# Six steps of a fused scan and feed-forward kernel: eight products in place of seven, the halves of y placed round them, and a chunk's first transposes moved

## The chip, the cores and the metric

The kernel runs on one core of a Trainium2 chip. Its time is the device time of one execution in microseconds (us), the median over several runs. A separate execution is recorded by the hardware profiler; all views below come from that one. The engines are TensorE (PE; its weight loads are shown apart as PEld), VectorE (DVE), ScalarE (ACT), GpSimd (POOL) and SyncE (SP, which here only issues DMAs). Each engine works through its own queue in the order in which the program emitted the instructions, and waits where an operand is not ready or a buffer is not free.

## The reference

Two blocks in a row. The first is a chunked state-space scan over 4 sequences of 8 heads, 768 positions, head width 32 and state width 16; the second is a feed-forward layer over the 3072 x 256 result.

```python
def _attn_ref(x, a, B, C):
    log_a = np.log(np.clip(a, 1e-06, 1.0))
    for c in range(nc):
        ...
        L = np.exp(cum[:, :, :, None] - cum[:, :, None, :]) * causal
        M = np.einsum('bhin,bhjn->bhij', Cc, Bc) * L
        y_intra = np.einsum('bhij,bhjd->bhid', M, xc)
        y_inter = np.einsum('bhin,bhnd->bhid', Cc, state) * decay_to_i[:, :, :, None]
        y[:, :, sl] = y_intra + y_inter
        ...
        state = decay_full[:, :, None, None] * state + np.sum(Bx, axis=2)

def _moe_ref(x, w_in, w_out):
    h = x @ w_in
    g = h * np.cos(h)
    return (g @ w_out).astype(np.float32)
```

d_model is 256 and d_ff 2048; everything is float32.

## The kernel before

**Steps and chunks.** The sequence is cut into 6 chunks of 128 positions (`NC = 6`). For each chunk the feed-forward layer runs 16 steps (`NF = 16`). Step n = 16c + f belongs to chunk c and place f. A step takes half of the chunk's rows (512 columns in all) and 256 of the 2048 hidden columns, computes h for them in one PSUM bank called `hp`, applies the cosine, and three steps later (`LAG = 3`) multiplies the gated result into the output accumulator `o`.

**One step's engines.** TensorE makes hp(n). ScalarE turns it to whole turns k (`wind_k`, L685), VectorE takes the rest w (`wind_w`, L691), ScalarE applies the sine (`gate`, L700), VectorE multiplies hp by it and writes gT (`gated`, L705). After that hp's bank may be written again. From n = 16 on, POOL forms differences gd of gT's quarters (`differ`, L730 to L733). The output product of step n (`seven(n)`, L849) uses seven products of 128 x 128 blocks instead of eight, after Strassen's scheme in Winograd's form, with gT, gd and prepared differences of w_out.

**Seven or eight products for hp.** `first(n)` (L678) makes hp with four matmuls of 256 columns, as much work as eight products of 128. `begin7(n)` (L778) makes it with seven: three products first; then ScalarE copies three parts (`copies`, L782 and L783); then two more products (`rest7[n][0]`), which wait for the copies; then VectorE adds the parts up (`sums` within it, L786 and L788); the last two products (`rest7[n][2]`) are made in the next step, behind the sums. They need differences of w_in (`wid`, POOL, L749) and of y (`differ_y`, POOL, L760). Before the change the steps in `sevens`, n = 33 to 93, all use seven.

**The order in such a step** is written out in `period7(n)`. On TensorE: `begin7(n)`, the first two products of `seven(n - 3)`, the last two hp products of n - 1, the middle part of `seven`, `rest7[n][0]`, the rest of `seven`. On VectorE: `wind_w(n - 1)`, the sums of n, `gated(n - 1)`, and then whatever `scan_work(c, f)` hands over as `extra`. A step that does not use seven, but is followed by one that does, leaves its `gate` and `gated` to the next step (`late`).

**PSUM.** There are eight banks: two for `o`, two tagged "h" used in turn by hp, and two pairs (`pair`) used by the scan. `bank_of(n)` says which steps take a bank of a pair for hp instead of an "h" bank: a third bank, f in (2, 6, 9, 10, 15) for chunks 2 to 4. Two steps that follow each other in the list of "h" users use different banks, and the next one waits for the first of them to be released.

**The scan in between.** While chunk c is in the feed-forward layer, chunk e = c + 1 is scanned, piece by piece. The pieces are: transposing blocks of B and C (`turn_blocks`, L585, VectorE), masking C (`mask_c`, L592, ScalarE), decays along the positions (`reaches`, L575, and `decays0`, L376, scans on VectorE), C weighted by them (`reach_c`, tile rT, L597), the products of C and B (`inner2`, L614, TensorE, into both pairs), their weighting by the decays (`weights`, tile m, L466, VectorE, one call for a quarter), the products of state and C (`open2`, L628, into both pairs again as ys), the sums for the next state (`sums2`, L478), the products with x (`finish2(e, (k,))`, L643, for the half k of the chunk), their copy to yT (`take_y`, L652, ScalarE), and the state's update (`add_state`, L501 for part 0, L503 for part 1). `sums2`, `take_ahead` (L490) and the decay scans of chunk e + 1 do not exist for the last chunk, e = 5. `open2` uses the states after half-chunks 2e - 1 and 2e, and `add_state(2e, (1,))` makes the second.

**Where the pieces stand.** `visits(n, e)` gives step f = 5 `inner2` ahead of everything on TensorE and three of four `weights` ahead of `wind_w`; step f = 12 `open2`; step f = 13 `sums2` ahead, `finish2(e, (0,))` in the middle, and two quarter scans. Step f = 14 has `finish2(e, (1,))` ahead. `scan_work` holds the rest; for c = 2 it has a list of its own, since chunk 3's first transposes stand at f = 0 there.

Of the kernel before, what the change touches and what calls it, by code (L numbers as in the profile page):

```python
# [25 lines left out]
def kernel(  # L26
# [18 lines left out]
    NC = S // P  # L45
    DM, DF = moe_w_in.shape
    KT = DM // P
    NF = DF // P
# [1022 lines left out]

    sevens = range(2 * NF + 1, NC * NF - 2)
    late = set()

    def bank_of(n):

        c, f = divmod(n, NF)
        third = n % 3 == 1 if c == NC - 1 else f in (2, 6, 9, 10, 15)  # L1080
        return pair("hp")[:, 0] if third else bank([P, TB], "hp", "h")

    def gates(n):
# [8 lines left out]
        gate(n)  # L1092
        gated(n)

    def period7(n, extra=(), begin=(), mid=(), early=(), o_first=False):

        first_, then, last_ = seven(n - LAG)
        for do in begin:
            do()
        if o_first:  # L1100
            first_()
        begin7(n, bank_of(n))
        while finished:
            finished.pop()()
        if not o_first:
            first_()
        if n - 1 in sevens:
            rest7[n - 1][2]()
            wind_k(n - 1)
        for do in mid:  # L1110
            do()
        then()
        rest7[n][0]()
        for do in early:
            do()
        if n - 1 in sevens:
            wind_w(n - 1)
        rest7[n][1]()
        if n - 1 in sevens or n - 1 in late:
            gate(n - 1)  # L1120
            gated(n - 1)
        last_()
        for do in extra:
            do()
# [53 lines left out]
    for n in range(AHEAD, 2 * NF):  # L1178
        c, f = divmod(n, NF)
        if n < NC * NF:  # L1180
# [33 lines left out]
            if joins:  # L1214
# [5 lines left out]
            behind += [lambda at=at: turn_blocks(*at) for at in chunks_at(n, "turn")]  # L1220
            behind += [lambda k=k, p=p: decays0(k, p) for k, at in unit_at.items()
                       for p in range(2) if at[0][p] == n]
            behind = [lambda k=2 * c + i, q=q: weights(k, q) for c, i in chunks_at(n, "weigh")
                      for q in range(2)] + behind
            behind = [lambda k=k: weights(k, 1) for k in units_at(n - 1, 3)] + behind
# [49 lines left out]
            sums2(c + 1)  # L1275
        load_more(n)

    def visits(n, e):

        f = n % NF  # L1280
        if f == 5:
            return dict(o_first=True, begin=[lambda: inner2(e)],
                        early=[lambda: weights(2 * e, 0), lambda: weights(2 * e + 1, 0),
                               lambda: weights(2 * e, 1)])
        if f == 12:
            return dict(mid=[lambda: open2(e)])
        if f == 13:
            return dict(o_first=True, begin=[lambda: sums2(e), lambda: take_ahead(e)],
                        mid=[lambda: finish2(e, (0,)), lambda: take_y(e, 0)] + [
                            lambda i=i: differ_y(e, i, G, slice(0, 1)) for i in range(4)],  # L1290
                        early=[lambda i=i: half_decay(2 * e + 3, 0, i)
                               for i in range(2 if e < NC - 1 else 0)])
        return {}

    def half_decay(k, p, i):

# [7 lines left out]
    def scan_work(c, f):  # L1304
# [6 lines left out]
                3: [lambda: reaches(e, 1), lambda: mask_c(e, 1, 1)],  # L1311
                4: [lambda: reach_c(e, 0), lambda: reach_c(e, 1)],
                6: [lambda: weights(2 * e + 1, 1), lambda: add_state(2 * e, (0,))],
                7: [lambda: add_state(2 * e, (1,))],
                11: [lambda: turn_blocks(e + 1, 0, (1,))],
                12: [lambda: turn_blocks(e + 1, 0, (0,))]}
        for i in range(2 if e < NC - 1 else 0):
            work.setdefault(13 + i, []).append(lambda i=i: half_decay(2 * e + 3, 1, i))
        if c == 2:
            work[0] = [lambda: add_state(5), lambda: turn_blocks(e, 0)]  # L1320
            work[1] = [lambda: turn_blocks(e, 1, (1,)), lambda: mask_c(e, 0, 0),
                       lambda: mask_c(e, 0, 1)]
            work[2] = [lambda: turn_blocks(e, 1, (0,)), lambda: mask_c(e, 1, 0),
                       lambda: mask_c(e, 1, 1)]
            work[3] = [lambda: reaches(e, 0)]
            work[4] = [lambda: reaches(e, 1)]
            work[6] = [lambda: weights(2 * e + 1, 1), lambda: reach_c(e, 0)]
            work[7] = [lambda: add_state(2 * e, (0,))]
            work[8] = [lambda: reach_c(e, 1)]
            work[9] = [lambda: add_state(2 * e, (1,))]  # L1330
        for i in range(4 if e < NC - 1 else 0):
            work.setdefault(7 + i, []).append(lambda i=i: half_decay(k, i // 2, i % 2))
        if e == NC - 1:
            for i in (11, 12, 15):
                work.pop(i)
        return work.get(f, [])

    for n in range(2 * NF, NC * NF + LAG):
# [9 lines left out]
        if n >= NC * NF:  # L1348
            second(n - LAG)
        elif n in sevens:  # L1350
            at = visits(n, e) if live else {}
            if f == 14 and c >= 2 and c < NC - 1:
                at = dict(o_first=True, begin=[lambda: finish2(e, (1,)), lambda: take_y(e, 1)])
            period7(n, extra, **at)
        else:
            first(n, rest7[n - 1][2] if n - 1 in sevens else None, to_=bank_of(n))
            if n - 1 in sevens:
                gates(n - 1)
            wind(n)
            for do in extra[:1]:  # L1360
                do()
            shut(n)
            for do in extra[1:]:
                do()
            second(n - LAG)
# [40 lines left out]
```

## Time and profile before

| what | value |
|---|---|
| median of 3 runs | 363.54 us (363.39 to 363.96) |
| the profiled execution, whole | 364.01 us |
| its span from first to last instruction | 361.6 us |
| TensorE matmul, steps with seven products, mean length of one instruction | 277 ns (two instructions to a product) |
| matmul of `first`, 256 columns | 383 ns |
| w, VectorE (L691) | 687 ns |
| k, ScalarE (L685) | 598 ns |
| sine, ScalarE (L700) | 722 ns |
| gT, VectorE (L705) | 686 ns |
| gd on POOL, first of three (L730) | 804 ns |
| granted TensorE clock | 1.0 throughout |

A line of the timeline gives the start and the length in us, then the engine, the source line, the operation, the tile written and the tiles read, the shape, and how many instructions are merged; in square brackets, how long the engine had been idle and what ended that. In the view by window, a line gives the window in us, its length, then busy us and instruction counts of PE, PEld, DVE, ACT and POOL, the granted clock, the share of the DMA engines and GB/s. TensorE's bars overlap, so its waits are read from the distance between starts.

### The profile page before, as it was taken

The numbers are of one execution on the slowest core, as the hardware profiler recorded it, in microseconds if no ns is written. First come the engines' busy times: TensorE is split into PE (matmuls) and PEld (weight loads), VectorE is DVE, ScalarE is ACT, GpSimd is POOL, SyncE is SP. The second block draws the span as 40 slices with busy tenths as digits, with TensorE's granted clock in tenths as the row PEclk, the third lists the DMA queues.
The fourth block names the chain that finished last, engine by engine and source line by source line (L and its number), as shares of the span: only waits on it lengthen the run. The fifth ranks groups of instructions, "written<-read, shape, count | busy, mean of one in ns | idle before, by whom it ended". The sixth has DMA issues, their size and how long they took to land.

```text
span 361.6 us, 10733 instructions
## 1 busy us (share of the span) xinstructions
PE 353.6 (98%) x4268; PEld 329.6 (91%) x4268; DVE 273.4 (76%) x479; ACT 213.0 (59%) x446; POOL 251.9 (70%) x410
## 2 busy tenths in 40 slices
PE   7999999999999999999999999999999999999995
PEld 4788888889989999998999999999999989999995
DVE  7789998478777847989868888868887536666663
ACT  3587766544455357456656656666746746666651
POOL 6567757879869987974866865766775674685671
PEclk9999999999999999999999999999999999999999
DMA  7996947692676129021319212101001001001011
GB/s 143 293 344 142 221 93 122 114 127 60 131 107 112 40 62 133 17 54 33 73 35 132 33 25 52 23 14 29 0 2 32 2 2 33 2 0 31 2 29 29
DMA packets 97328, 26.46 MB, mean 73 GB/s; under 512 B 87328, under 2 KB 93184, under 8 KB 97280
## 3 DMA queue, kind: packets, MB, share of 16 engines
q1 hardware_dynamic: 96032, 25.41, 35.0%
q8 instruction: 33, 0.54, 0.6%
q10 hardware_dynamic: 1248, 0.39, 0.5%
q14 instruction: 15, 0.12, 0.1%
HBM read 22.38 MB, written 3.34 MB: 71 GB/s over the span
## 4 chain that ended last, share of the span: by engine, by line
PE 81%; DVE 10%; ACT 4%; issue 1%; DMA 1%; POOL 1%; SPq 0%; DVEq 0%; POOLq 0%; ACTq 0%
PE o L849 28%; PE hp L778 21%; PE hp L678 17%; PE o L808 7%; DVE w L691 2%; DVE gT L705 2%; ACT w L700 2%; PE y L643 2%; DVE m L466 1%; DMA bc<-in_B_dram 1%; DVE rT L597 1%; DVE lam L376 1%; ACT k L685 1%; PE y L628 1%; PE y L478 1%
## 5 line engine op out<-in xcount | busy, mean ns | idle before, releaser
L700 ACT ACTIVATE w<-w,quarter 128x512 f32<-128x512 f32 x96 | 69.3, 722 | 67.9 <-DVE w L691 67.4
L730 POOL TENSOR_TENSOR gd<-gT 128x256 f32<-128x256 f32 x79 | 63.5, 804 | 65.3 <-DVE gT L705 53.1
L691 DVE SCALAR_TENSOR_TENSOR w<-hp,k 128x512 f32<-128x512 f32 x96 | 65.9, 687 | 55.8 <-ACT k L685 55.2
L685 ACT ACTIVATE k<-hp 128x512 int32<-128x512 f32 x96 | 57.4, 598 | 35.0 <-PE hp L678 25.3
L705 DVE TENSOR_TENSOR gT<-hp,w 128x512 f32<-128x512 f32 x96 | 65.9, 686 | 16.0 <-ACT w L700 10.4
L849 PE MATMUL o<-words,gd 128*128 128x128 f32 x474 | 76.6, 277 | 0.0
L678 PE MATMUL hp<-yT,w_in 128*128 128x256 f32 x280 | 66.8, 383 | 0.3 <-DVE gT L705 0.3
L849 PEld LDWEIGHTS o<-words,gd 128*128 128x128 f32 x474 | 64.1, 192 | 0.5
L778 PE MATMUL hp<-m,wid 128*128 128x128 f32 x366 | 61.7, 277 | 0.2 <-ACT hp L783 0.2
L678 PEld LDWEIGHTS hp<-yT,w_in 128*128 128x128 f32 x280 | 51.4, 190 | 8.0 <-POOL mag L250 0.7
L778 PEld LDWEIGHTS hp<-m,wid 128*128 128x128 f32 x366 | 50.6, 192 | 0.7 <-ACT hp L783 0.3
L849 PE MATMUL o<-w_out,gT 128*128 128x128 f32 x316 | 50.1, 277 | 0.2 <-issue 0.2
L778 PE MATMUL hp<-yT,w_in 128*128 128x128 f32 x244 | 47.2, 275 | 0.4 <-DVE gT L705 0.4
L849 PEld LDWEIGHTS o<-w_out,gT 128*128 128x128 f32 x316 | 43.3, 192 | 1.9 <-issue 0.5
L732 POOL TENSOR_TENSOR gd<-gT,gd 128x128 f32<-128x128 f32 x79 | 39.6, 501 | 6.2
L733 POOL TENSOR_TENSOR gd<-gT,gd 128x128 f32<-128x128 f32 x79 | 37.9, 480 | 6.2
L778 PEld LDWEIGHTS hp<-yT,w_in 128*128 128x128 f32 x244 | 37.0, 192 | 0.6 <-issue 0.6
L782 ACT COPY m<-hp 128x256 f32<-128x256 f32 x61 | 22.4, 367 | 17.2 <-PE hp L778 16.4
L849 PE MATMUL o<-words,gT 128*128 128x128 f32 x158 | 30.5, 275 | 0.0
L849 PE MATMUL o<-w_out,gd 128*128 128x128 f32 x158 | 30.5, 275 | 0.0
L376 DVE TENSOR_TENSOR_SCAN lam<-arow,unit 128x256 f32<-128x256 f32 (+1 forms) x28 | 30.4, 1090 | 0.0
L808 PE MATMUL o<-w_out,gT 128*128 128x256 f32 x128 | 29.9, 379 | 0.0
(126 smaller groups left out, 553.8 us busy)
## 6 DMA issues: line engine op xcount, KB each, us to landing
words<-in_moe_w_in_dram SPq DMA_DIRECT2D x8, 512.0 KB
words<-in_moe_w_out_dram SPq DMA_DIRECT2D x8, 512.0 KB
xr<-in_x_dram SPq DMA_DIRECT2D x24, 128.0 KB
arow<-a_cut SPq DMA_DIRECT2D x10, 256.0 KB
arow<-a_cut SPq DMA_DIRECT2D x10, 252.0 KB
out_dram<-sum SPq DMA_DIRECT2D x18, 128.0 KB
bc<-in_B_dram SPq DMA_DIRECT2D x24, 64.0 KB
along<-a_all SPq DMA_DIRECT2D x8, 65.0 KB
```

Source lines behind the costliest of these rows:

```text
L376: V.tensor_tensor_scan(out=lams[k][:, p, hs].rearrange(flat), data0=rows_.rearrange(flat), data1=unit0[:, hs].rearrange(flat), initial=0.0 ...
L678: PE.matmul(to_[:, e], lhsT=w_in[:, k, fs], rhs=y[:, k], start=(k == 0), stop=(k == KT - 1), skip_group_check=True)
L685: ACT.activation(k, hp[n], AF.Copy, bias=0.25, scale=INV_2PI)
L691: V.scalar_tensor_tensor(out=w, in0=hp[n], scalar=INV_2PI, in1=k, op0=ALU.mult, op1=ALU.subtract)
L700: ACT.activation(cos, cos, AF.Sin, bias=quarter, scale=TWO_PI)
L705: V.tensor_tensor(out=gT[n], in0=hp.pop(n), in1=cos, op=ALU.mult)
L730: G.tensor_tensor(out=d[:, 0:2], in0=g[:, 1:2].to_broadcast([P, 2, P]), in1=g[:, 3::-3], op=ALU.subtract)
L732: G.tensor_tensor(out=d[:, 2], in0=g[:, 0], in1=d[:, 0], op=ALU.subtract)
L733: G.tensor_tensor(out=d[:, 3], in0=g[:, 2], in1=d[:, 2], op=ALU.subtract)
L778: PE.matmul(at[:, i], lhsT=w[q], rhs=y_[q], start=(q == 1), stop=True, skip_group_check=True)
L808: PE.matmul(o[c, u][:, t], lhsT=g[:, 2 * e + t], rhs=w_out[:, 2 * j + e], start=(j == e == t == 0), stop=(j == NJ - 1 and e == 1), skip_gr ...
L849: PE.matmul(at[q], lhsT=a_[q], rhs=w[q], start=(j == 0 and q in starts), stop=(j == NJ - 1), skip_group_check=True)
```

## The change

Six steps, f = 5 and f = 13 in chunks 2 to 4, leave `sevens`. They get functions of their own, `visit_g` and `visit_y`, which replace `visits` and the arguments of `period7`. In `visit_y` both halves of `finish2` stand round the step's own `first`, and the decay scans of f = 13 and f = 14 become two whole ones. `add_state(2e, (1,))` moves from f = 7 (f = 9 for c = 2) to the end of f = 11. Chunk 3's first two transposes move to steps 29 and 30, behind `gated`, and most of c = 2's own list goes. The third bank is taken at f in (2, 7, 10, 15).

```diff
+    visited = [NF * c + f for c in range(2, NC - 1) for f in (5, 13)]
+    sevens = [n for n in range(2 * NF + 1, NC * NF - 2) if n not in visited]
-    sevens = range(2 * NF + 1, NC * NF - 2)
...
-        third = n % 3 == 1 if c == NC - 1 else f in (2, 6, 9, 10, 15)
+        third = n % 3 == 1 if c == NC - 1 else f in (2, 7, 10, 15)
...
-    def period7(n, extra=(), begin=(), mid=(), early=(), o_first=False):
+    def period7(n, extra=(), mid=()):
...
+            if n in (2 * NF - 3, 2 * NF - 2):
+                behind.append(lambda k=2 * NF - 2 - n: turn_blocks(3, 0, (k,)))
...
+    def visit_g(n, e):
+
+        inner2(e)
+        rest7[n - 1][2]()
+        wind_k(n - 1)
+        second(n - LAG)
+        weights(2 * e, 0)
+        wind_w(n - 1)
+        weights(2 * e, 1)
+        gate(n - 1)
+        gated(n - 1)
+        first(n, to_=bank_of(n))
+        weights(2 * e + 1, 0)
+        gates(n)
+
+    def visit_y(n, e):
+
+        halves = [lambda p=p: decays2(2 * e + 3, p) for p in range(2 if e < NC - 1 else 0)]
+        sums2(e)
+        take_ahead(e)
+        rest7[n - 1][2]()
+        wind_k(n - 1)
+        second(n - LAG)
+        finish2(e, (0,))
+        first(n, to_=bank_of(n))
+        for do in halves[:1]:
+            do()
+        wind_w(n - 1)
+        gate(n - 1)
+        gated(n - 1)
+        for do in halves[1:]:
+            do()
+        take_y(e, 0)
+        for i in range(4):
+            differ_y(e, i, G, slice(0, 1))
+        finish2(e, (1,))
+        gates(n)
+        take_y(e, 1)
...
-                7: [lambda: add_state(2 * e, (1,))],
...
-        for i in range(2 if e < NC - 1 else 0):
-            work.setdefault(13 + i, []).append(lambda i=i: half_decay(2 * e + 3, 1, i))
         if c == 2:
-            work[0] = [lambda: add_state(5), lambda: turn_blocks(e, 0)]
-            work[1] = [lambda: turn_blocks(e, 1, (1,)), lambda: mask_c(e, 0, 0),
-                       lambda: mask_c(e, 0, 1)]
-            work[2] = [lambda: turn_blocks(e, 1, (0,)), lambda: mask_c(e, 1, 0),
-                       lambda: mask_c(e, 1, 1)]
-            work[3] = [lambda: reaches(e, 0)]
-            work[4] = [lambda: reaches(e, 1)]
-            work[6] = [lambda: weights(2 * e + 1, 1), lambda: reach_c(e, 0)]
-            work[7] = [lambda: add_state(2 * e, (0,))]
-            work[8] = [lambda: reach_c(e, 1)]
-            work[9] = [lambda: add_state(2 * e, (1,))]
+            work[0] = [lambda: add_state(5), lambda: reaches(e, 0)]
+            work[1] += [lambda: mask_c(e, 0, 0), lambda: mask_c(e, 0, 1)]
...
+        work.setdefault(11, []).append(lambda: add_state(2 * e, (1,)))
...
-            period7(n, extra, **at)
+            period7(n, extra, [lambda: open2(e)] if live and f == 12 else ())
+        elif live and f == 5:
+            visit_g(n, e)
+        elif live and f == 13:
+            visit_y(n, e)
```

`decays2(k, p)`, which `visit_y` calls, is `decays0(k, p)` for a whole half of the heads' rows and, after the second, the load of a later decay row (`load_arow`, SP) and `weigh0` (L382, POOL). `second(n)` emits all seven products of `seven(n)` in a row.

More of the change, by code (lines that the diff above doesn't have):

```diff
@@ L1093, in shut @@
         gated(n)
-    def period7(n, extra=(), begin=(), mid=(), early=(), o_first=False):
[L1097 to L1101, printed above, removed]
+    def period7(n, extra=(), mid=()):
         begin7(n, bank_of(n))
@@ L1104, in period7 @@
             finished.pop()()
-        if not o_first:
-            first_()
+        first_, then, last_ = seven(n - LAG)
+        first_()
         if n - 1 in sevens:
@@ L1113, in period7 @@
         rest7[n][0]()
-        for do in early:
-            do()
         if n - 1 in sevens:
@@ L1276 @@
         load_more(n)
[L1278 to L1293, printed above, removed]
+    def visit_g(n, e):
[33 more added lines that the diff above has]
+        take_y(e, 1)
     def half_decay(k, p, i):
@@ L1350 @@
         elif n in sevens:
-            at = visits(n, e) if live else {}
-            if f == 14 and c >= 2 and c < NC - 1:
-                at = dict(o_first=True, begin=[lambda: finish2(e, (1,)), lambda: take_y(e, 1)])
-            period7(n, extra, **at)
+            period7(n, extra, [lambda: open2(e)] if live and f == 12 else ())
[3 more added lines that the diff above has]
+            visit_y(n, e)
         else:
```

## The prediction

> **What bounds the kernel now.** Steps are named by n = 16c + f (chunk c, place f). I read the page's engine shares first, then busy time by chunk, then the timeline of single steps.
>
> ```profile
> PE 353.6 (98%) x4268; PEld 329.6 (91%) x4268; DVE 273.4 (76%) x479; ACT 213.0 (59%) x446; POOL 251.9 (70%) x410
> ...
> PE 81%; DVE 10%; ACT 4%; issue 1%; DMA 1%; POOL 1%; SPq 0%; DVEq 0%; POOLq 0%; ACTq 0%
> ```
>
> ```profile
> 142.07:199.55 57.48, 56.87 (x771) 54.91 (x769) 48.05 (x89) 35.35 (x82) 41.19 (x71) 1.00 0.36 61
> 199.55:256.03 56.48, 56.01 (x771) 54.73 (x769) 46.69 (x88) 35.63 (x82) 38.10 (x66) 1.00 0.13 27
> 256.03:312.02 55.99, 55.27 (x707) 53.94 (x705) 38.10 (x74) 34.00 (x75) 35.15 (x65) 1.00 0.05 11
> 312.02:343.29 31.27, 31.27 (x283) 31.27 (x282) 20.22 (x40) 20.58 (x44) 21.03 (x40) 1.00 0.05 10
> ```
>
> TensorE sets the end. Its 98% hides waits, because a matmul's bar (277 ns) is longer than the distance to the next (0.11 us), so I count distances between starts. The last window holds ten undisturbed steps: 31.27 / 10 = 3.127 us, fourteen products, **0.223 us each**. Sixteen such steps are 50.03. The first three windows (the work of steps 35 to 82) hold 7.45, 6.45 and 5.96 us more. The scan's small matmuls, with the seams around them, explain 5.56 of it (step 53's `inner2` 1.34, step 60's `open2` 1.13, step 61's `sums2` 1.13, `finish2` 0.98 twice; chunk 4 has no `sums2`). What is left, 1.9, 0.9 and 1.5 us, is waiting, and only that can be won.
>
> Step 53 (f = 5) and the start of 54:
>
> ```profile
> 206.05 0.69 DVE L705 TENSOR_TENSOR gT<-hp,w 128x512 f32<-128x512 f32 x1 [0.19 <-POOL gd L733]
> ...
> 206.66 1.60 DVE L597 TENSOR_TENSOR rT<-turned,reach 128x256 f32<-128x256 f32 x2
> ...
> 208.18 1.87 DVE L466 TENSOR_TENSOR m<-g,lam 128x512 f32<-128x512 f32 x3
> ...
> 209.97 0.67 DVE L691 SCALAR_TENSOR_TENSOR w<-hp,k 128x512 f32<-128x512 f32 x1
> ...
> 211.02 0.30 DVE L788 TENSOR_TENSOR hp<-hp,m 128x128 f32<-128x128 f32 x1
> ...
> 211.37 0.49 PE L778 MATMUL hp<-yT,wid 128*128 128x128 f32 x2 [0.29 <-DVE hp L788]
> ```
>
> DVE is busy from 206.05 to 211.32 nearly without a break; TensorE, due at 210.92 for step 53's last two products, waits for the sums, 0.56 us with the weight load that could not run ahead. Together with 0.10 in step 53 itself the visit loses 0.66. Chunk 4 is alike; in chunk 2 the `rT` work lies elsewhere and only 0.11 is lost.
>
> **The change, part by part** (on chunk 3 unless named).
>
> *The eighth product.* Four 256-wide products take 1.73 us (132.12 to 133.85), seven take 1.56: +0.17 at each of six visits.
>
> *The step after a visit.* It has no last two products of its predecessor between its own first three and the two that need ScalarE's copies. Step 33, which follows an eight-product step today, shows the price:
>
> ```profile
> 136.69 0.25 ACT L783 COPY hp<-hp 128x128 f32<-128x128 f32 x1
> ...
> 137.08 0.46 PE L778 MATMUL hp<-m,wid 128*128 128x128 f32 x2
> ```
>
> Due at 136.97, it starts at 137.08 and its second half comes 0.07 late: +0.18, six times.
>
> *The visit at f = 5, a new wait.* With f = 6 taken off the third-bank list, f = 3, 4, 5, 6 share two banks, so step 54's first product needs hp(52)'s bank, free once `gated(52)` has run. That such a reuse blocks TensorE is shown in chunk 4, where f = 13 takes f = 11's bank:
>
> ```profile
> 290.06 0.68 DVE L705 TENSOR_TENSOR gT<-hp,w 128x512 f32<-128x512 f32 x1
> ...
> 290.88 0.46 PE L778 MATMUL hp<-yT,w_in 128*128 128x128 f32 x2 [0.42 <-DVE gT L705]
> ```
>
> DVE's queue: `rT` twice to 208.25 (as now), `weights` 0.67 to 208.85, `w(52)` to 209.47 (its `k` is ready by 207.8), `weights` to 210.07, the sine 0.72 from 209.51 to 210.23, `gated(52)` 210.33 to 211.02; TensorE starts 0.15 later (as at 290.88) with a 0.07 seam: 211.24. TensorE's own work: 205.23 + 1.34 (`inner2`) + 2 products 0.45 + 7 products 1.56 + 1.73 = 210.30. Wait 0.94; the two sums (0.72 on DVE) and the 0.66 disappear. Per visit +0.17 + 0.18 + 0.94 - 0.66 = **+0.63** in chunks 3 and 4; chunk 2 gets chunk 3's order of `rT` and loses only its own 0.11: **+1.18**. Sum +2.44. Queued behind are `weights(2e+1,0)`, `w(53)` and `gated(53)`, done by 215.0; the next reader of that bank is step 56, at 217. Bounds: 0 if `gated(52)` came 0.9 earlier, 1.3 if POOL stretches one more DVE operation.
>
> *`add_state(2e,(1,))` from f = 7 to the end of f = 11.* `open2` in step 60 reads what it writes, in its second half (k = 1):
>
> ```profile
> 230.71 0.65 DVE L585 STREAM_TRANSPOSE turned<-blocks 128x256 f32<-128x256 f32 x1
> ...
> 230.78 1.00 PE L628 MATMUL y<-rT,state 32*64 32x64 f32 x64
> ...
> 230.94 0.74 POOL L730 TENSOR_TENSOR gd<-gT 128x256 f32<-128x256 f32 x1
> ```
>
> The add comes behind the transpose, at 231.27, while POOL's L730 runs until 231.68. The same add beside L730 today:
>
> ```profile
> 191.13 0.77 POOL L730 TENSOR_TENSOR gd<-gT 128x256 f32<-128x256 f32 x1 [0.43 <-DVE gT L705]
> 191.35 0.83 DVE L503 TENSOR_TENSOR state<-state,whole 128x256 f32<-128x256 f32 x1
> ```
>
> It ends 0.28 after POOL's; beside an idle POOL (218.22) it takes 0.41. So it ends near 231.96, and the half due at 231.17 starts near 231.99: **+0.82**. Chunk 2 likewise (half due 174.80, L730 ends 175.59, start 175.91): **+1.11**. In chunk 4 no transpose stands before it, the add ends at 287.60, and the half is due at 287.65: 0. Bounds: 0.5 if POOL gave way; 1.2 if all of `open2` waited.
>
> The Trainium skill, "SBUF — State Buffer", section "Who interferes with whom", says that a VectorE operation with two SBUF inputs and a reading GpSimd operation block each other whole, by order of issue. By that rule the add would take its full 0.41 after 231.68 and the wait would be 0.95; the row shows 0.28 behind POOL's end, so part of the add overlaps, and I keep the row.
>
> *The visit at f = 13.* TensorE's small matmuls and seams stay equal in number. Lost today: 0.11 in step 62 (241.61 to 241.83 for a distance of 0.11). New: 0.17 + 0.18. Step 62 takes hp(60)'s bank, but `gated(60)` ends near 239 and TensorE gets there near 240.8, since `finish2(e,(1,))` now stands ahead. The two whole scans (1.21 to 1.38 each in steps 28 and 30) lie before and after `w(60)` inside those 1.8 us; were that cover gone, each would cost up to its length. Chunk 3 +0.24, chunk 2 +0.24. Chunk 4 has no `sums2`: it saves the 0.65 of the line at 290.88 and 0.11, but step 76's last products now come first in step 77, due at 289.85 with sums ending 290.15: 0.45 with the seam. +0.04. With the adds: 1.35 + 1.06 + 0.04 = **+2.45**. `take_y`, `differ_y`, `weigh0` and the `arow` load (SP, issued one step sooner, used a chunk later) have all of steps 62 and 63: 0. On POOL `weigh0` now waits for the second scan ahead of `differ_y`, whose readers start at f = 0: 0.
>
> *Chunk 3's first transposes.* Two of 0.64 go behind `gated(29)` and `gated(30)`, where DVE idles 0.43 and 0.89 us before its next `w`; the sums between them give way 0.2. TensorE there needs neither: 0, at most +0.6. Their blocks were issued by 109.3, 14 us before. `reaches(3,0)` comes at 136.3 in place of two transposes, its row loads issued 12.7 us before: 0. What it wins lies in chunk 2:
>
> ```profile
> 142.02 0.89 ACT L592 ACTIVATE cT<-turned,slot 128x256 f32<-128x256 f32 x2
> ...
> 143.20 0.25 ACT L783 COPY hp<-hp 128x128 f32<-128x128 f32 x1
> ...
> 143.50 0.49 PE L778 MATMUL hp<-m,wid 128*128 128x128 f32 x2 [0.15 <-ACT hp L783]
> ```
>
> One of two masks leaves ScalarE's queue ahead of the copies: -0.45. In steps 40 to 42 DVE is the bound (steps of 3.44, 3.60, 3.61); without `rT` and the adds they become chunk 3's 3.13: -1.26. Together **-1.71**.
>
> **Sum:** 2.44 + 2.45 - 1.71 = +3.18. The profiled execution (span 361.6, 364.01 with what lies around it) becomes 367.2; it stood 0.47 above the median of the runs, 363.54, so I forecast **366.7**.
>
> **Rivals.**
> A, *DVE's queue runs ahead* (faster): freed of the sums, DVE stands 0.9 us earlier against TensorE, so that `gated(52)` is out by 210.3 and the add done by 231.2. Then 2.82 and 1.93 fall away: 3.18 - 4.75 = -1.6, 362.0; it decides once two thirds of the lead are there. For it: DVE has 0.72 less in each visit. Against: the sums stand behind `gated(52)`'s forerunners, which are not shortened.
> B, *one of the waits is missing*: without the bank wait 363.9, without the `open2` wait 364.8. For it: I infer both orders from the code. Against: the line at 290.88.
> C, *the waits are longer*: all of `open2` waits (+0.4 at each visit), and POOL stretches DVE's queue at f = 5 by 0.3: 366.7 + 2.1 = 368.8. For it: second `rT` 0.94 against 0.64. Against: parts of one tile are waited for apart, as w_in is read at 51.37 while POOL still writes another part until 51.74.
> D, *the change is only its products*: 6 x 0.17 = 1.0, 364.5, if every wait merely changes its name.
>
> **Chances.** Forecast 0.64 (own range 365.4 to 367.8), A 0.08, B 0.14 (half near no change), C 0.08, D 0.06. The 8-in-10 range takes the forecast's own, most of B and D: **364.5 to 367.9**. The measurement tells 0.2% (0.73 us) from nothing: faster 0.09, same 0.07, slower 0.84.
>
> **What would show it.** Step 54's first product waiting for `gT` L705, about 0.9, three times; `y` L628 broken in two in chunks 2 and 3, its wait on L503; step 77 starting on L788; 0.18 after each visit; steps 40 to 42 at 3.13. I am wrong if `gated(52)` comes before TensorE needs the bank, or if the add is ahead of the transpose.

## The result and the profile after

The changed kernel is slower, as forecast: median 366.14 us (365.54 to 368.20, nine runs) against 363.96 us (363.39 to 365.98, nine runs) of the kernel before, ratio 1.0067 [1.0044, 1.0091]. The forecast was 366.7, the range 364.5 to 367.9. The profiled execution took 366.07 us with a span of 364.3; the span grew by 2.66 us.

The page's shares, after: first the engines' busy time, then the chain that ended last.

```profile
PE 354.5 (97%) x4232; PEld 328.2 (90%) x4232; DVE 269.9 (74%) x463; ACT 210.0 (58%) x434; POOL 252.2 (69%) x410
...
PE 73%; DVE 10%; ACT 5%; SPq 4%; POOL 3%; issue 2%; DMA 2%; DVEq 0%; POOLq 0%; ACTq 0%
```

There are 36 matmuls, 16 DVE and 12 ACT instructions fewer, and the span is longer. The matmuls are no work saved: a visit makes `hp` in 8 matmuls of 256 columns in place of 14 of 128, and the 8 take 0.17 us more. On DVE and ACT work was removed (the sums and copies of six visits; in two chunks four half scans became two whole ones). New waits came on TensorE. In the chain TensorE fell from 81% to 73%, and SP's queue, which was at 0%, has 4%. This piece of the chain, in chunk 2, is where SP comes in:

```profile
170.32 3.95 DMA arow<-a_cut
...
174.29 0.64 DVE turned L585
174.93 0.61 DVE state L503
...
175.59 0.49 PE y L628 x32
```

The last three lines are a real chain of waiting: TensorE waits for the state's update, and that stands behind a transpose. The step from the transpose back to a DMA is not: the transpose starts 0.60 us after the start of the `gT` ahead of it on DVE (173.69), the distance at which DVE follows a `gT` wherever it has work waiting (211.14 to 211.75 in step 53), and it reads `blocks`, not `arow`. The chain took the semaphore event that came last, and followed SP's issues back from there.

Busy time by chunk, in the columns explained before, with windows set by the same output products as before:

```profile
142.32:200.36 58.04, 56.47 (x758) 54.24 (x757) 45.53 (x82) 34.40 (x78) 41.69 (x71) 1.00 0.30 56
200.36:258.14 57.78, 56.48 (x758) 54.25 (x757) 45.16 (x82) 34.41 (x78) 38.45 (x66) 1.00 0.12 26
258.14:314.65 56.51, 55.62 (x694) 53.55 (x693) 36.82 (x70) 33.00 (x71) 35.21 (x65) 1.00 0.05 11
314.65:345.92 31.27, 31.27 (x283) 31.27 (x281) 20.23 (x40) 20.60 (x44) 21.09 (x40) 1.00 0.04 10
```

The three chunks take 0.56, 1.30 and 0.52 us more; the ten undisturbed steps at the end take 31.27 as before. Which waits are new stands in the view of waits, TensorE alone, 140 to 346 us (total, number, longest; the weight load's share is not in them):

```profile
PE hp L778 <- DVE gT L705: 2.4, 3, 1.0
PE y L628 <- DVE state L503: 1.2, 2, 0.6
PE hp L778 <- DVE hp L788: 0.2, 1, 0.2
```

Before, this view had 1.0 us of waits for the sums (L788), four times, and 0.4 for `gT`, once. Two of the forecast's three signatures are here by name: the bank three times, and `open2`'s wait for the state twice, in chunks 2 and 3. The third is the last line.

The bank wait, steps 53 and 54, on the timeline:

```profile
208.13 0.95 DVE L597 TENSOR_TENSOR rT<-turned,reach 128x256 f32<-128x256 f32 x1
...
209.00 0.68 DVE L466 TENSOR_TENSOR m<-g,lam 128x512 f32<-128x512 f32 x1
...
209.60 0.68 DVE L691 SCALAR_TENSOR_TENSOR w<-hp,k 128x512 f32<-128x512 f32 x1
...
211.14 0.69 DVE L705 TENSOR_TENSOR gT<-hp,w 128x512 f32<-128x512 f32 x1 [0.26 <-ACT w L700]
...
211.98 0.46 PE L778 MATMUL hp<-yT,w_in 128*128 128x128 f32 x2 [0.70 <-DVE gT L705]
...
213.63 0.49 PE L778 MATMUL hp<-m,wid 128*128 128x128 f32 x2
```

`gated(52)` stands behind `rT`, `weights`, `w` and `weights` in DVE's queue and ends at 211.83. Its own last wait is for the sine (0.26 us idle, "<-ACT w L700"), and the sine comes after `w`. So it is what stands ahead of `w` in the queue that makes it late; the second `weights` fits into the time of the sine. `first(53)` started at 209.39, and its eight instructions take 1.73, so step 54's first product is due at 211.12; it starts at 211.98, 0.15 after `gT`'s end. With 0.07 lost at its second half (the seam), 0.93 us are lost. In chunk 2 the same wait is 1.12 (due 153.07, start 154.19) and the seam 0.07.

The last line shows the price of the copies: the product starts 0.01 late, its second half another 0.10 later.

`open2` in step 60:

```profile
232.08 0.64 DVE L585 STREAM_TRANSPOSE turned<-blocks 128x256 f32<-128x256 f32 x1
232.13 0.63 PE L628 MATMUL y<-rT,state 32*64 32x64 f32 x32
...
232.30 0.73 POOL L730 TENSOR_TENSOR gd<-gT 128x256 f32<-128x256 f32 x1
232.56 0.76 DVE L503 TENSOR_TENSOR state<-state,whole 128x256 f32<-128x256 f32 x1
...
233.37 0.49 PE L628 MATMUL y<-rT,state 32*64 32x64 f32 x32 [0.60 <-DVE state L503]
...
233.79 0.49 PE L849 MATMUL o<-words,gd 128*128 128x128 f32 x2
```

Before, 64 matmuls ran in one piece from 230.78 to 231.71. Now the first 32 run, the others stand until the add is through, and the next product comes at 233.79: 1.66 us in place of 0.93.

In step 77 the two last products of step 76 stand ahead of all else, and wait for the sums:

```profile
292.30 0.39 PE L849 MATMUL o<-w_out,gd 128*128 128x128 f32 x2
...
292.87 0.49 PE L778 MATMUL hp<-yT,wid 128*128 128x128 f32 x2 [0.19 <-DVE hp L788]
```

Due at 292.52, they start at 292.87, and their second product 0.11 late: 0.46.

All further counts are distances between the starts of the first output products of steps, so that every stretch begins and ends at the same work. "f = 5" is the three steps that hold that visit, "f = 13" the three that hold `open2` and that visit.

| stretch, us | before | after | add back at f = 7 | w first | both | add first |
|---|---|---|---|---|---|---|
| chunk 2, step 35 and its neighbour | 6.73 | 6.33 | 6.33 | 6.33 | 6.33 | 6.33 |
| chunk 2, f = 5 | 10.83 | 12.21 | 12.19 | 11.61 | 11.62 | 12.20 |
| chunk 2, steps 39 to 43 | 16.90 | 15.63 | 15.78 | 15.63 | 15.78 | 15.63 |
| chunk 2, f = 13 | 13.63 | 14.47 | 13.84 | 14.46 | 13.74 | 13.76 |
| chunk 3, f = 5 | 11.40 | 11.95 | 11.94 | 11.34 | 11.34 | 11.94 |
| chunk 3, f = 13 | 13.71 | 14.46 | 13.74 | 14.45 | 13.74 | 13.77 |
| chunk 4, f = 5 | 11.40 | 11.95 | 11.93 | 11.34 | 11.34 | 11.94 |
| chunk 4, f = 13 | 13.25 | 13.21 | 13.21 | 13.21 | 13.21 | 13.21 |
| span | 361.6 | 364.3 | 363.0 | 362.9 | 360.6 | 362.3 |

After less before: f = 5 +1.38, +0.55 and +0.55 (together +2.48), f = 13 +0.84, +0.75 and -0.04 (+1.55), moves -0.40 and -1.27 (-1.67). These sum to +2.36; of the span's remaining 0.30, 0.33 lies ahead of step 19, before any changed step, and chunk 1 gives back 0.08. In the 14 traces of this case the time ahead of step 19 goes from 80.89 to 81.66 us and chunk 1 from 57.70 to 58.58, so a few tenths in a span mean nothing by themselves; the stretches of the table are the safer measure.

### The profile page after: what moved, and what is told of

The parts are those of the page before. It is cut to its first block, busy times and chain, and to the rows that moved or that the text cites. A ratio compares the mean times of both kernels' runs of the same rounds, so it can differ in the third digit from the quotient of the medians.

```text
span 364.3 us, 10622 instructions
## 1 busy us (share of the span) xinstructions
PE 354.5 (97%) x4232; PEld 328.2 (90%) x4232; DVE 269.9 (74%) x463; ACT 210.0 (58%) x434; POOL 252.2 (69%) x410
## 4 chain that ended last, share of the span: by engine, by line
PE 73%; DVE 10%; ACT 5%; SPq 4%; POOL 3%; issue 2%; DMA 2%; DVEq 0%; POOLq 0%; ACTq 0%
PE o L849 25%; PE hp L678 18%; PE hp L778 16%; PE o L808 7%; DVE gT L705 3%; ACT w L700 2%; DVE w L691 2%; PE y L643 2%; SPq L188 2%; DVE rT L597 1%; POOL gd L730 1%; ACT k L685 1%; DMA arow<-a_cut 1%; DMA bc<-in_B_dram 1%; PE y L478 1%
## 5 line engine op out<-in xcount | busy, mean ns | idle before, releaser
L730 POOL TENSOR_TENSOR gd<-gT 128x256 f32<-128x256 f32 x79 | 64.0, 810 | 66.9 <-DVE gT L705 56.4
L700 ACT ACTIVATE w<-w,quarter 128x512 f32<-128x512 f32 x96 | 69.5, 724 | 65.3 <-DVE w L691 65.2
L678 PE MATMUL hp<-yT,w_in 128*128 128x256 f32 x328 | 78.5, 383 | 0.4 <-DVE gT L705 0.4
L849 PE MATMUL o<-words,gd 128*128 128x128 f32 x474 | 75.3, 276 | 0.0
L678 PEld LDWEIGHTS hp<-yT,w_in 128*128 128x128 f32 x328 | 60.0, 190 | 9.2 <-POOL mag L250 0.7
L778 PE MATMUL hp<-m,wid 128*128 128x128 f32 x330 | 55.7, 278 | 0.0
L778 PEld LDWEIGHTS hp<-m,wid 128*128 128x128 f32 x330 | 45.6, 192 | 0.3
L778 PE MATMUL hp<-yT,w_in 128*128 128x128 f32 x220 | 43.0, 277 | 2.4 <-DVE gT L705 2.4
L778 PEld LDWEIGHTS hp<-yT,w_in 128*128 128x128 f32 x220 | 33.4, 192 | 3.8 <-PE hp L678 3.5
L786 DVE TENSOR_TENSOR hp<-hp,m 128x256 f32<-128x256 f32 x55 | 23.3, 424 | 12.6 <-PE hp L778 8.3
L782 ACT COPY m<-hp 128x256 f32<-128x256 f32 x55 | 20.3, 369 | 19.3 <-PE hp L778 19.0
```

What stands on the lines that cost most here:

```text
L678: PE.matmul(to_[:, e], lhsT=w_in[:, k, fs], rhs=y[:, k], start=(k == 0), stop=(k == KT - 1), skip_group_check=True)
L700: ACT.activation(cos, cos, AF.Sin, bias=quarter, scale=TWO_PI)
L730: G.tensor_tensor(out=d[:, 0:2], in0=g[:, 1:2].to_broadcast([P, 2, P]), in1=g[:, 3::-3], op=ALU.subtract)
L778: PE.matmul(at[:, i], lhsT=w[q], rhs=y_[q], start=(q == 1), stop=True, skip_group_check=True)
L786: V.tensor_tensor(out=at[:, 2:0:-1], in0=at[:, 1:2].to_broadcast([P, 2, P]), in1=parts, op=ALU.add)
L849: PE.matmul(at[q], lhsT=a_[q], rhs=w[q], start=(j == 0 and q in starts), stop=(j == NJ - 1), skip_group_check=True)
```

## The experiments

### The two waits, one at a time and together

The changed kernel with the state's update back at f = 7:

```diff
-        work.setdefault(11, []).append(lambda: add_state(2 * e, (1,)))
+                7: [lambda: add_state(2 * e, (1,))],
```

> The changed kernel with add_state(2e,(1,)) back at f = 7. Theory (the add behind the transpose at f = 11 holds open2's second half): open2 of steps 44 and 60 runs in one piece again (0.9 to 1.0 us from its first to the next large product, where the changed kernel has 1.66), step 76 is unchanged, nothing else moves: 1.4 us less than the changed kernel, about 0.4% over the kernel before. Rival (what is late comes next: the sums of step 60 or sums2 wait instead): 0 to 0.3 us less than the changed kernel, about 0.6% over before.

Measured: 364.60 against 363.88, ratio 1.0019 [1.0006, 1.0032], span 363.0. The wait for L503 is gone from the view of waits, `open2` runs in one piece, and f = 13 falls by 0.63 and 0.72 us in chunks 2 and 3 and by nothing in chunk 4. (Chunk 2's has 0.10 of a slower `finish2` in it, of which more in the last section; with both edits it falls by 0.73.) In chunk 2 the add costs 0.15 in steps 39 to 43, where DVE is short of time. The bank wait is untouched (2.3, three times).

The changed kernel with `wind_w(n - 1)` ahead of the first `weights` of `visit_g`, and one `weights` behind `gated`:

```diff
-        weights(2 * e, 0)
         wind_w(n - 1)
-        weights(2 * e, 1)
+        weights(2 * e, 0)
         gate(n - 1)
         gated(n - 1)
         first(n, to_=bank_of(n))
+        weights(2 * e, 1)
         weights(2 * e + 1, 0)
```

> The changed kernel with wind_w(n - 1) ahead of the weights at f = 5, one weights inside the sine's time and the other two behind first. Theory (step 54 waits for the PSUM bank that gated(52) frees, and gated(52) is late by VectorE's queue alone): gated(52) ends 0.6 us sooner against TensorE, the wait at step 54's first product falls from 0.93 to about 0.3 in each of three chunks: 1.8 us less than the changed kernel, about 0.2% over before. Rival (the bank was not what held it, or ScalarE's copies take the wait over): under 0.4 us less than the changed kernel.

Measured: 364.30 against 363.88, ratio 1.0010 [0.9995, 1.0025], span 362.9: no longer told apart from the kernel before. Each f = 5 gets 0.60 or 0.61 us shorter. DVE's order in step 53, and TensorE's start, in this kernel:

```profile
208.88 0.68 DVE L691 SCALAR_TENSOR_TENSOR w<-hp,k 128x512 f32<-128x512 f32 x1
209.49 0.67 DVE L466 TENSOR_TENSOR m<-g,lam 128x512 f32<-128x512 f32 x1
...
210.42 0.69 DVE L705 TENSOR_TENSOR gT<-hp,w 128x512 f32<-128x512 f32 x1 [0.26 <-ACT w L700]
...
211.26 0.46 PE L778 MATMUL hp<-yT,w_in 128*128 128x128 f32 x2
```

One `weights`, 0.6 from its start to the next instruction's, no longer stands ahead of `w`, and TensorE stood 0.60 less. `gT` waits 0.26 for the sine here too, so the `weights` that is left between `w` and `gT` costs nothing. So it is DVE's queue up to `w` that sets this wait, instruction by instruction, with the sine behind it. Some 0.3 us remain.

Both edits together:

> Both of these edits in the changed kernel. Theory: the two waits are independent and add up: 3.2 us less than the changed kernel, so 0.1 to 0.2% under the kernel before. Rival (one of the waits hides behind the other): no more than 2 us less than the changed kernel, still over before.

Measured: 362.88 against 363.88, ratio 0.9964 [0.9942, 0.9987], span 360.6. The savings add up: 1.81 at f = 5 and 1.45 at f = 13. With all its eighth products, and two pieces of DVE's work put elsewhere, the change is faster than the kernel before. What cost the change its gain was mainly two places in DVE's queue, not the products.

### The place of the add or its order

The add stays at f = 11, but ahead of the transpose:

```diff
-        work.setdefault(11, []).append(lambda: add_state(2 * e, (1,)))
+        work.setdefault(11, []).insert(0, lambda: add_state(2 * e, (1,)))
```

> The changed kernel with the two pieces of f = 11 in the other order: add_state(2e,(1,)) first, then the transpose. Theory (the add is late only because the transpose, and then POOL's first gd, stand before it): it starts 0.5 us sooner, before POOL takes gd, ends about when open2's second half is due, and open2 takes 0.95 to 1.1 us in chunks 2 and 3 instead of 1.66: 1.2 us less than the changed kernel, with the add still at f = 11. Rival (f = 11 is too late in itself, as the add cannot start before gated(58)): at most 0.4 us less than the changed kernel.

Measured: 364.89 against 364.05, ratio 1.0020 [1.0005, 1.0034], span 362.3. f = 13 falls by 0.71 and 0.69, as much as with the add at f = 7, and steps 39 to 43 stay at 15.63. Step 60 in this kernel:

```profile
230.89 0.55 DVE L503 TENSOR_TENSOR state<-state,whole 128x256 f32<-128x256 f32 x1
...
230.95 1.03 PE L628 MATMUL y<-rT,state 32*64 32x64 f32 x64
...
231.12 0.92 POOL L730 TENSOR_TENSOR gd<-gT 128x256 f32<-128x256 f32 x1
231.36 0.64 DVE L585 STREAM_TRANSPOSE turned<-blocks 128x256 f32<-128x256 f32 x1
```

The add ends at 231.44, just when `open2` gets to its second half (230.95 + 0.5). Now POOL's L730 is the later one, and it takes 0.92 in place of 0.73. So the delay was the order of two instructions in one list, not the step to which the add was moved.

### The eighth product at f = 5 alone

The kernel before, with f = 5 alone changed (the third-bank list, too):

```diff
+    visited = [NF * c + 5 for c in range(2, NC - 1)]
+    sevens = [n for n in range(2 * NF + 1, NC * NF - 2) if n not in visited]
-    sevens = range(2 * NF + 1, NC * NF - 2)
...
-        third = n % 3 == 1 if c == NC - 1 else f in (2, 6, 9, 10, 15)
+        third = n % 3 == 1 if c == NC - 1 else f in (2, 7, 10, 15)
...
+        elif live and f == 5:
+            visit_g(n, e)
```

> The kernel before with eight products at f = 5 alone (visit_g and the third-bank list of the change; f = 13, the transposes and the adds stay as before). Theory: in chunks 3 and 4 +0.55 us each (0.17 product, 0.12 copies, 0.93 bank wait, less 0.66), in chunk 2, whose rT work stands elsewhere, a bank wait of about 0.4 and +0.55: 1.6 us over before, 0.45%. Rival (an eighth product costs only itself): 0.5 us over before.

Measured: 364.90 against 363.88, ratio 1.0025 [1.0008, 1.0041], span 363.1. f = 5 takes 11.33, 11.94 and 11.94 us: +0.50, +0.54 and +0.54, +1.58 in all. The view of waits has the bank three times (1.8 us in total, 0.7 the longest). In chunk 2 the wait is shorter, since one decay scan of 1.03 us stands in DVE's queue where chunks 3 and 4 have `rT` twice: step 38's first product, due at 153.40, starts at 153.66, and 0.07 follow. With the eighth product (0.17), the copies (0.11) and the 0.11 that fall away this is its 0.50. Steps 39 to 43 give 0.17 back (16.73 for 16.90), since DVE comes to them with a lead (step 40's `gT` starts 0.17 sooner against TensorE). So the visit loses by itself, without the other moves: some 1.4 us.

### The gains alone, and from there to a faster kernel

The kernel before, with only the moves: two transposes at steps 29 and 30, chunk 2's own list gone, and with it the add at f = 7 in chunk 2.

```diff
+            if n in (2 * NF - 3, 2 * NF - 2):
+                behind.append(lambda k=2 * NF - 2 - n: turn_blocks(3, 0, (k,)))
...
+            work[0] = [lambda: add_state(5), lambda: reaches(e, 0)]
+            work[1] += [lambda: mask_c(e, 0, 0), lambda: mask_c(e, 0, 1)]
```

> The kernel before with only chunk 3's first transposes at steps 29 and 30 and chunk 2's scan work in chunk 3's order. Theory: steps 40 to 42 fall to 3.13 us (-1.26), step 35 loses its wait for the copies (-0.40), chunk 2's f = 5 takes over chunk 3's order of rT and its wait (+0.57): 1.1 us under before, 0.3%. Rival (the two transposes cost VectorE's time in chunk 1): 0 to 0.5 us under before, with steps 29 to 31 longer.

Measured: 364.31 against 365.15, ratio 0.9980 [0.9955, 1.0006]: not told from no change. This one missed its expectation. Chunk 2 gains 0.48 (step 35 -0.40, f = 5 +0.84, steps 39 to 43 -0.94). I had left out two things. First, steps 39 to 43 take 0.33 more than in the changed kernel (15.96 and 15.63). The add at f = 7 is 0.15 of that, by the changed kernel with the add back (15.78). The other 0.18 is the lead of DVE that the visit with eight products leaves, as with f = 5 alone changed (0.17). Second, the `rT` work, now at f = 4 in chunk 2, meets a later POOL, which prepares `wid` there:

```profile
149.87 0.72 POOL L894 TENSOR_TENSOR sum<-ps,sum 128x256 f32<-128x256 f32 x1
...
149.95 1.80 DVE L597 TENSOR_TENSOR rT<-turned,reach 128x256 f32<-128x256 f32 x2
...
150.56 0.91 POOL L749 TENSOR_TENSOR wid<-w_in,wid 128x256 f32<-128x256 f32 x1
```

The pair takes 1.80 here and 1.60 in chunk 3. Each `rT` ends 0.28 or 0.29 us after the operation of POOL beside it, here the first after L894 (ends 150.60) and the second after `wid` (151.47). In chunk 3 L894 ends 1.05 us after the start of the `gT` ahead, here 1.25, so the first `rT` takes 0.93 in place of 0.73. POOL has `wid` work more in its queue in chunk 2; that this makes it later is inferred. The visit takes 11.67 us, not chunk 3's 11.41. The change pays the same (1.79 for the pair): its chunk 2 loses 0.2 more at f = 5 than the forecast had.

So the next kernel moves one `rT` (`reach_c(e, 0)`) from f = 4 to f = 1:

```diff
-                1: [lambda: turn_blocks(e, 1, (1,))],
+                1: [lambda: turn_blocks(e, 1, (1,)), lambda: reach_c(e, 0)],
...
-                4: [lambda: reach_c(e, 0), lambda: reach_c(e, 1)],
+                4: [lambda: reach_c(e, 1)],
```

> The same with reach_c(e,0) moved from f = 4 to f = 1. Theory (at f = 5 with seven products TensorE waits for sums that are late by VectorE's queue): the queue is 0.6 us shorter there, the wait of 0.56 at f = 6's two last products of f = 5 goes in three chunks: 1.7 us under b1_sooner, 2.8 us under before. Rival (f = 1 becomes the bound, 0.65 + 0.64 behind 2.1 us of the step's own): under 0.6 us less than b1_sooner.

Measured: 362.97 against 365.15, ratio 0.9948 [0.9913, 0.9983], span 360.4. (The kernel before scattered widely in this round, from 363.58 to 368.79, so the span, 1.2 us under the 361.6 of before, says more here than the ratio.) f = 5, still with seven products, takes 10.88, 10.84 and 10.84: 0.79, 0.57 and 0.57 less than with the moves alone. At f = 1 chunks 3 and 4 pay 0.20 (6.53 in place of 6.33).

Then chunk 4's f = 13, where the kernel before already has a bank wait: in the last chunk `finish2(e, (0,))` comes ahead of step 77's own work, in place of `sums2`, which that chunk lacks.

```diff
-            return dict(o_first=True, begin=[lambda: sums2(e), lambda: take_ahead(e)],
-                        mid=[lambda: finish2(e, (0,)), lambda: take_y(e, 0)] + [
+            last = e == NC - 1
+            half = [lambda: finish2(e, (0,)), lambda: take_y(e, 0)]
+            return dict(o_first=True, begin=half if last else
+                        [lambda: sums2(e), lambda: take_ahead(e)],
+                        mid=([] if last else half) + [
```

> The same with finish2(5,(0,)) ahead of step 77's own first products, where chunks 2 and 3 have sums2. Theory: it fills the 0.65 us in which step 77 waits for the bank of step 75: 0.65 us under b2_rT, 3.4 us under before, about 0.95%. Rival (the wait only moves to a later product of that step): no difference to b2_rT.

Measured: 362.63 against 365.15, ratio 0.9939 [0.9914, 0.9964], span 360.2: not told apart from the kernel before it. The bank wait is gone from the view of waits, but chunk 4's f = 13 takes 13.69 us, not less than 13.25. In the middle of `finish2` TensorE pauses, and "issue" means that the profile shows nothing that released it:

```profile
288.06 0.79 PE L643 MATMUL y<-m,xr 64*32 64x64 f32 x57
289.28 0.31 PE L643 MATMUL y<-m,xr 64*32 64x64 f32 x7 [0.42 <-issue]
```

The same kernel, run once more:

> b3_ch4 once more, for the like wait of 0.64 us at 288.64 to 289.28: the same two readings. In the first chunk 4's f = 13 takes 13.7 us again, in the second about 13.1.

Measured: 362.00 against 364.44 in one run each, span 360.1. This time the view shows `finish2` as one piece:

```profile
288.39 1.16 PE L643 MATMUL y<-m,xr 64*32 64x64 f32 x64
```

Still, its 64 matmuls take 1.08 us to the next product, where 0.79 is usual. The pause is there again, only shorter: from the start of the 57th matmul to that of the 58th the trace has 0.27 us, where the first run has 0.64 and an undisturbed `finish2` 0.01. And step 78 takes 4.32 us in both runs, where 4.01 is usual, so part of the bank wait went one step further. f = 13 takes 13.31: the move gains nothing.

The last two kernels keep what paid. The first has seven products at f = 5 as before, the changed kernel's `visit_y` at f = 13, the moves, and DVE's scan work spread: `rT` (`reach_c(e, 0)`) at f = 0 (f = 1 for c = 2), `reaches` at f = 15 of the chunk before, `add_state(2e + 1)` at f = 14.

```diff
+    visited = [NF * c + 13 for c in range(2, NC - 1)]
...
+        work = {14: [lambda: add_state(2 * e + 1)],
+                15: [lambda: reaches(e + 1, 0), lambda: mask_c(e + 1, 0, 0)],
+                0: [lambda: reach_c(e, 0), lambda: mask_c(e, 0, 1)],
...
+                4: [lambda: reach_c(e, 1)],
...
+        elif live and f == 13:
+            visit_y(n, e)
```

> Seven products at f = 5 as before, f = 13 as in the change, the transposes sooner, add_state(2e,(1,)) at f = 7, add_state(2e+1) at f = 14, reaches(e+1,0) at f = 15, reach_c(e,0) at f = 0 (f = 1 for chunk 3), so that no step before f = 5 has more than one of VectorE's pieces. Theory: the wait of 0.56 at f = 5 is gone in three chunks without the 0.2 us that b2_rT pays at f = 1 in chunks 3 and 4: span near 359.6, 2 us under the kernel before, 0.6 us under b2_rT. Rival (the update at f = 14 meets the sums of the step after the visit, or f = 15 and f = 0 become late): no better than b2_rT.

Measured: 361.90 against 364.05, ratio 0.9936 [0.9914, 0.9958], span 359.9. f = 5 takes 10.86, 10.84 and 10.85, f = 1 no longer pays, and the view of waits between 140 and 346 us has a single line of 0.2 us. f = 13 takes 13.96, 13.74 and 13.21: the eighth product there costs about its own 0.17 in chunks 2 and 3. (Before: 13.63, 13.71 and 13.25. In chunk 2, 0.18 of the 0.33 is a slow `finish2`; in chunk 3 the trace of before has a pause of its own of 0.14, and with f = 5 alone changed, where that is missing, f = 13 took 13.58.)

The second also puts `finish2(e, (0,))` ahead of step 76's last products in chunk 4's `visit_y`, so that the sums have 0.8 us more:

```diff
         take_ahead(e)
+        if e == NC - 1:
+            finish2(e, (0,))
         rest7[n - 1][2]()
...
-        finish2(e, (0,))
+        if e < NC - 1:
+            finish2(e, (0,))
```

> The same, with finish2(5,(0,)) ahead of step 76's last two products in step 77, which has no sums2. Theory: it covers the 0.45 us in which step 77 waits for step 76's sums: 0.45 us under h1_spread, in chunk 4's f = 13 alone. Rival (as in b3_ch4, a wait of about 0.6 appears inside finish2 and takes it back): no gain over h1_spread.

Measured: 361.63 against 364.05, ratio 0.9931 [0.9907, 0.9955], span 359.8: faster than both kernels, not told apart from the one before it. Chunk 4's f = 13 falls from 13.21 to 12.75, as expected; but chunk 2's, where no instruction was moved, rises from 13.96 to 14.54, by a pause inside `finish2`:

```profile
181.76 0.69 PE L643 MATMUL y<-m,xr 64*32 64x64 f32 x45
182.94 0.41 PE L643 MATMUL y<-m,xr 64*32 64x64 f32 x19 [0.49 <-issue]
```

Run again:

> h2_last once more, for the wait of 0.7 us that its trace shows at 182.24 to 182.94 inside finish2, released by nothing that the profile shows. If it belongs to the order of TensorE's instructions, it is at the same instruction again and chunk 2's f = 13 takes 14.5 us; if it is chance of one execution, it is gone and chunk 2's f = 13 takes 13.8 to 14.0.

Measured: 361.54 against 364.44 in one run each, span 359.6. The pause is there again, as long as before and after the same 45 matmuls. But it is not this kernel's alone. In the kernel with spread scan work, which is the same program up to there, the 46th matmul of this burst also starts late, by 0.16 us where 0.01 is usual. So the pause was there before the edit; why it is 0.71 in both runs of this kernel and 0.16 in the other, no run shows.

## Why the prediction was right, and where its sum was 0.8 too high

The forecast's case was right, and none of the rivals'. Its sum for the span was +3.18, the same stretches measured +2.36.

**f = 5: +2.44 forecast, +2.48 measured.** The wait is the bank's, it comes three times, and 0.93 against 0.94 is its size. It stands where DVE's queue puts it: taking one 0.60 out of the queue ahead of `w` moved it by 0.60. That the sums agree so well is in part luck, since two small errors cancel. The copies after this visit cost 0.11, not 0.18. And chunk 2 lost +1.38, not +1.18: there the two `rT` take 0.93 and 0.94 us, in chunk 3 0.72 and 0.95, since POOL, with `wid` work in its queue, is 0.2 later beside the first. This bit of rival C (POOL stretching DVE's queue) holds in one chunk of three, as far as the overlap shows; no run has the one without the other.

**The wait in `open2`: +1.11 and +0.82 forecast, 0.67 and 0.73 measured.** Mechanism and halves are right, and chunk 4 is spared as forecast. In chunk 3 the add ends 0.28 us after POOL's L730 (233.03 to 233.31; the nominal end, 232.56 + 0.76, is 233.32), the very distance that the row from f = 9 gave. The size was off in chunk 2, and this is the term that was mis-sized: "L730 ends 175.59" was read from the trace of before, where L730 started 0.48 us after `open2` (174.86 and 174.38). In the changed kernel it starts 0.18 after it (174.53 and 174.35), as in chunk 3. Before and after:

```profile
174.38 1.05 PE L628 MATMUL y<-rT,state 32*64 32x64 f32 x64
...
174.86 0.73 POOL L730 TENSOR_TENSOR gd<-gT 128x256 f32<-128x256 f32 x1
```

```profile
174.35 0.63 PE L628 MATMUL y<-rT,state 32*64 32x64 f32 x32
...
174.53 0.73 POOL L730 TENSOR_TENSOR gd<-gT 128x256 f32<-128x256 f32 x1
```

Before, the gT's of the slow steps ahead came late, and POOL's queue with them; the moves that shorten those steps bring POOL forward. Two kernels show this: with the moves alone L730 starts 0.16 after `open2` (174.76 and 174.60), with f = 5 alone changed still 0.48 (175.40 and 174.92). The forecast gave the moves their gain in TensorE's time, and kept POOL where it had been. That is the largest single error, 0.44 us.

The Trainium skill, "SBUF — State Buffer", section "Who interferes with whom", has the two operations block each other whole. By it the add would have ended 0.41 after L730's end; the measured 0.28 is nearer the row that the forecast kept, and each `rT` beside POOL in step 53 and its like in chunk 2 ends 0.28 or 0.29 after POOL's operation, too. When the add was put first, L730 became the slower one, 0.92 for 0.73, which fits the section's order of issue, though L730 ended 0.60 after the add, not its whole 0.73.

**f = 13 without the adds: +0.24 each forecast in chunks 2 and 3, 0.02 in chunk 3 and 0.17 in chunk 2 measured; chunk 4 +0.04 forecast, -0.04 measured.** The +0.17 of the eighth product is there. The copies cost 0.11, which is what step 62 had lost to them before, so they add nothing; I had subtracted 0.11 and added 0.18. That leaves 0.17, which is what chunk 2 has. In chunk 3 the trace of before was itself slow, by a pause behind `sums2`:

```profile
233.69 0.64 PE L478 MATMUL y<-xr,sc 64*32 64x64 f32 x35
234.50 0.60 PE L849 MATMUL o<-w_out,gT 128*128 128x128 f32 x4 [0.18 <-issue]
```

Counted with the matmuls ahead of these lines, `sums2` and its seams took 1.13 us there, and 0.99 in the changed kernel; 0.17 - 0.14 is chunk 3's 0.02 to within 0.01. The pause is no matter of the products that follow. With f = 5 alone changed they follow in the same order, and there is none:

```profile
234.54 0.86 PE L478 MATMUL y<-xr,sc 64*32 64x64 f32 x64
235.33 0.71 PE L849 MATMUL o<-w_out,gT 128*128 128x128 f32 x4
```

So 0.14 of the 0.8 by which the sum was too high lies in the trace of before, not in the change.

**Chunk 4's f = 13.** The wait for L788 is 0.46 with its seam, 0.45 forecast; it takes the place of the bank wait at 290.88 of the trace before, as forecast.

**Moves: -1.71 forecast, -1.67 measured** (step 35 -0.40 of -0.45, steps 39 to 43, where DVE was the bound, -1.27 of -1.26). That the copies no longer stand behind two masks, and that these steps become chunk 3's, is right. But 0.17 of the -1.27 belongs to the visit at f = 5, by the kernel with that alone (16.73 for 16.90). What the transposes cost at steps 29 and 30 is nothing that can be seen: chunk 1 takes 57.94 us against 58.02.

**From the span to the median.** The spans differ by 2.66, the medians of nine by 2.18: of the execution, 2.40 us lay outside the span before (364.01 - 361.61) and 1.80 after (366.07 - 364.27), and the forecast had kept this equal. It had also set out from the median of three, 363.54, where the median of nine is 363.96. So the forecast's time is nearer (366.7 and 366.14) than its difference (3.18 and 2.18), and that is luck: a start 0.42 too low met a sum that was too high.

**Rivals.** *A* (DVE ahead, no wait) is out: the queue was behind, not ahead. What it supposed, `gated(52)` out earlier and the add done in time, is what the two edits together largely make, and there the time does fall below the kernel before: 0.9964. *B* (one wait missing) is out by the view of waits, but its two prices were near: without the bank wait 363.9 and without `open2`'s 364.8 were forecast; putting `w` first, which leaves a third of the bank wait, gave 364.30, and the add elsewhere 364.60 and 364.89. *C* holds for 0.2 us in one chunk; `open2` was not held whole in any. *D* (products only) would be +1.0 of span in place of +2.66.

## What to carry over

An instruction that a reader waits for is worth ordering to the instruction: one short operation ahead of the other in the same list was worth 0.7 us a chunk here, and one `weights` 0.6, while an eighth product cost 0.17 a visit. Before a consumer is moved off its own buffer, or a buffer's list is changed, look up who releases the buffer that it then shares, and where that instruction stands in its queue. When the wait is computed, the other engine's times must be counted forward from the changed program, not read from the old trace.

## What was not expected of the chip

Bursts of 64 short matmuls (L643, 64 x 64) usually take 0.79 us to the next product, but 0.97 was seen (181.92 to 182.89 in the kernel with spread scan work), 1.08 in the repeated chunk 4 kernel, and 1.46 and 1.52 with a pause that nothing in the profile released.

The pauses have fixed places. Counted from the start of the trace, one comes after 2,243 matmuls: it takes 0.05 us with the moves alone, 0.09 with the add back at f = 7, 0.16 with spread scan work and 0.71 in both runs of the last kernel; elsewhere the step there is 0.01. One comes after 2,876, behind chunk 3's `sums2`, in the kernel before and in the three others that have as many matmuls up to there (0.18 to 0.54 from start to start, where 0.15 is usual). One comes after 3,637, in both runs of the chunk 4 kernel, with 0.64 and 0.27. So the place goes with the count of TensorE's instructions, and the length differs between kernels and between runs of one kernel. With the weight loads, 1,266 instructions lie from the first place to the second and 1,522 from the second to the third. The page has 33 transfers on a queue that it calls "instruction" (q8), of 16 KB each, for the 8,536 instructions of TensorE, 259 to a transfer; the two distances are 4.9 and 5.9 times that. This points to the supply of instructions to TensorE in a burst that uses them up fast. It is an estimate from counts, and no run here tests it.

A forecast that has such a burst on its path should allow up to 0.7 us more for it, and look whether the trace that it starts from has such a pause already.
